# One load of r per batch, six tokens to a partition, in a linear-attention and token-mixing kernel on one Trainium2 core

## The chip, the cores and the metric

The kernel runs on one core of a Trainium2 chip. The metric is the device time in microseconds (us) of one execution; a time of a kernel is the median of its runs. Three runs of the kernel before gave 136.98, 137.22 and 137.23 us.

## The reference

A linear attention with a decaying state (4 batches, 8 heads, 768 tokens, head size 48) gives x; a block that mixes tokens and channels follows. All in float32 at the interface.

```python
# attention, per batch b and head h; state is D x D, D = 48
for t in range(S):                       # S = 768
    cur     = einsum('bhd,bhe->bhde', u * k[t], v[t])
    y[t]    = einsum('bhd,bhde->bhe', r[t], state + cur)
    state   = w * state + einsum('bhd,bhe->bhde', k[t], v[t])
x = y.transpose(0, 2, 1, 3).reshape(B, S, H * D)          # 4 x 768 x 384
# mixing
theta = x @ w_theta                                        # 384 x 384
y  = w_tok_r @ (x * cos(theta)) + w_tok_i @ (x * sin(theta))   # 768 x 768 over tokens
u  = x + y
out = u + relu(u @ w_ch)                                   # 384 x 384
```

## The kernel before

**Tiles.** A batch's 768 tokens are three *pairs*, each of two chunks of 128 tokens; there are 12 pairs in all (g = 0 to 11). For the pairs 0 to 6 (`PAIRS`) k and v lie two tokens of a head to a partition, for the later ones one token to a partition, one DMA per chunk. r lies two tokens to a partition in every pair. A load of one tensor for one pair (384 KB in all) goes into one of 16 load buffers `ld` of 128 x 768 float32.

**Attention, `front(b)`.** Per pair: r and k are multiplied by powers of w, which takes them to a common origin of the decay (`Rw`, `Kw`, L554 and L556, 128 x 768; "decay" below). The powers themselves are exponentials on ScalarE at the start (`kpow`, `rpow`, `kpow_c`, L399; one instruction for each of the two tokens of a partition). The products are turned so that the head dimension lies on partitions: `flip` (L489) is a row of 128 x 128 matmuls against an identity into one PSUM bank (L493) and one copy out of it (L503 on ScalarE, L504 on VectorE) into `RT` or `KT`. `scores` (L605) are K by R per head, masked by VectorE into `mAT` (L614). `outer` (L671) gives a chunk's contribution to the state; F, T and N (L713 to L727) carry the state on, and its 16-bit copies are `Sb` or `Sd` (L684 to L707). `vb` is the 16-bit cast of v (L581 ScalarE, L583 VectorE, L585 POOL). `PD` (L621) is R times K elementwise, `diag` (L638) sums it with u, `dg` (L643) takes it out of PSUM, and `yd` (L647) is that times v: the term of the token itself. The output of a pair is `states` (L747, L799), `outputs` (L760, L812) and `bonus` (L776) summed in PSUM and copied to x (L784, L786, L821).

**Mixing, `front` and `mixing(b)`.** x is turned (`flip TX`, or a transposing DMA, L510); `theta` (L835) and cos and sin (L842, L846) and z = x times both (L850, VectorE). `mix` (L901) multiplies the turned token weights `WrT`, `WiT` with z, 12 matmuls of 384 columns for each 128 tokens; `un` (L919) adds x; u is turned by a transposing DMA (L510), `chan` (L929) multiplies with w_ch, ScalarE takes the relu out (L956), POOL adds u (L959), and one DMA per pair writes 384 KB out (L977). Token weights come by casting DMAs that POOL issues (L462, float32 to 16 bits) and are turned by `flip W`. For the last pair alone u is made turned (L876), and sums end on VectorE (L945, L964).

**Order.** Every step is a task of a `Plan`, with the engines that could do it ("ways") and their planned nanoseconds. The program's order of tasks, the way of each, the PSUM banks and some extra waits are tables written out in the file (`ORDER`, `WAYS`, `BANKS`, `AFTER`): a pair (a, b) in `AFTER` makes task b wait for the end of task a on another engine. Each engine, and the queue of SyncE (SP) that issues nearly all loads, stores and transposing DMAs, works through its own tasks strictly in that order. A DMA's plan entry has the queue, the packets per DMA engine and nanoseconds per packet, such as `desc=(0, 64, 26)`. `IDLE` puts matmuls on zeros (L293) behind chosen tasks on TensorE, 128 x 512 ("wide") or 128 x 128 ("narrow"); `WARM` puts some at the very start. Buffers are rings, and a task that writes a buffer waits for the last readers of it:

```python
NL, NR, NK, NV, NRT, NKT, NPD, NM, NSB, ND_ = 15 if KR_BY_DMA else 16, 2, 4, 6, 4, 3, 2, 5, 6, 3
...
def load(src, b, pr, what, pairs):
    i = nload[0] % NL
    nload[0] += 1
    rows = src[b, :, 2 * pr * C:(2 * pr + 2) * C, :]
    if pairs:
        P.add(sp(lambda: nc.sync.dma_start(
            out=Ls[i].rearrange("p (h n) -> p h n", h=H),
            in_=rows.rearrange("h (p j) d -> p h (j d)", j=2))), wr=[("L", i, 0), ("L", i, 1)],
            prio=-90 + 0.001 * nload[0], desc=(0, 64, 26), name="load " + what, kind="load")
```

## Time and profile before

| | |
|---|---|
| median of 3 runs | 137.22 us (136.98 to 137.23) |
| the profiled execution | 136.61 us, of which the span from first to last instruction is 134.8 us |
| granted TensorE clock | 0.997 |
| TensorE (PE) busy | 127.9 us, 95% of the span |
| VectorE (DVE), ScalarE (ACT), GpSimd (POOL) busy | 106.1, 81.0, 68.8 us |
| DMA | 25.47 MB in 67,199 packets, 61,801 of them under 512 B |

A row of a timeline has its start and length in us, then engine, source line, operation, output<-inputs by the program's tile names, shape and count; in brackets the idle time of the engine before it and what ended it. A row of the windows view has the stretch, its length, then per engine the busy us. Matmuls are pipelined, so the length of a row of TensorE contains a drain, and the distance from start to start is what one costs in a row of them. L numbers are lines of the kernel before; the changed file is longer.

### The profile page before, as it was taken

The numbers are of one execution on the slowest core, as the hardware profiler recorded it, in microseconds if no ns is written. First come the engines' busy times: TensorE is split into PE (matmuls) and PEld (weight loads), VectorE is DVE, ScalarE is ACT, GpSimd is POOL, SyncE is SP. The second block draws the span as 40 slices with busy tenths as digits, with TensorE's granted clock in tenths as the row PEclk, the third lists the DMA queues.
The fourth block names the chain that finished last, engine by engine and source line by source line (L and its number), as shares of the span: only waits on it lengthen the run. The fifth ranks groups of instructions, "written<-read, shape, count | busy, mean of one in ns | idle before, by whom it ended". The sixth has DMA issues, their size and how long they took to land.

```text
span 134.8 us, 4625 instructions
## 1 busy us (share of the span) xinstructions
PE 127.9 (95%) x1943; PEld 85.8 (64%) x1943; DVE 106.1 (79%) x201; ACT 81.0 (60%) x157; POOL 68.8 (51%) x76
## 2 busy tenths in 40 slices
PE   6999998899999999999999999899999999999970
PEld 1346666765776775876676776566667757667840
DVE  5099988687998999889798878799899997351370
ACT  3478696598968596684965153863731758900220
POOL 6003789295160456827326989664056955370220
PEclk9999999999999999999999999999999999999998
DMA  3999999999999955797999999979899950326344
GB/s 92 265 269 261 143 204 197 255 258 234 242 277 236 261 138 74 144 209 139 281 180 234 171 189 253 163 134 309 196 302 198 103 116 8 117 79 198 78 177 173
DMA packets 67199, 25.47 MB, mean 189 GB/s; under 512 B 61801, under 2 KB 67178, under 8 KB 67178
## 3 DMA queue, kind: packets, MB, share of 16 engines
q1 hardware_dynamic: 64744, 22.23, 76.3%
q0 software_dynamic: 2432, 2.95, 13.4%
q8 instruction: 15, 0.25, 0.8%
q14 instruction: 6, 0.05, 0.1%
q10 hardware_dynamic: 2, 0.00, 0.0%
HBM read 20.06 MB, written 4.72 MB: 184 GB/s over the span
## 4 chain that ended last, share of the span: by engine, by line
PE 78%; DVE 7%; DMA 5%; ACT 2%; POOL 2%; issue 2%; DVEq 0%; POOLq 0%; ACTq 0%
PE bank L901 31%; PE bank L493 11%; PE bank L835 8%; PE bank L929 7%; DMA uu_all<-uu_all 5%; PE bank L605 4%; PE bank L876 3%; PE bank L671 3%; PE bank L760 2%; PE bank L293 2%; DVE Rw L554 2%; PE bank L747 2%; PE bank L776 1%; PE bank L812 1%; PE bank L638 1%
## 5 line engine op out<-in xcount | busy, mean ns | idle before, releaser
L901 PE MATMUL bank<-z,WrT 128*128 128x384 bf16 x132 | 43.0, 326 | 0.0
L901 PE MATMUL bank<-z,WiT 128*128 128x384 bf16 x132 | 42.9, 326 | 0.0
L959 POOL TENSOR_TENSOR fin_all<-fin_all,uu_all 128x384 f32<-128x384 f32 x20 | 19.5, 992 | 22.7 <-ACT fin_all L956 8.7
L647 POOL TENSOR_TENSOR yd<-dg,vb 128x768 bf16<-128x768 f32 x10 | 14.7, 1471 | 11.8 <-DVE PD L621 5.1
L614 DVE TENSOR_TENSOR mAT<-bank,mask 128x512 bf16<-128x512 f32 x28 | 18.4, 682 | 0.3 <-PE bank L605 0.2
L901 PEld LDWEIGHTS <-WrT 128*128 128x128 bf16 x132 | 12.9, 98 | 7.7 <-issue 0.3
L956 ACT ACTIVATE fin_all<-bank 128x384 f32<-128x384 f32 x20 | 9.7, 494 | 12.9 <-issue 8.5
L901 PEld LDWEIGHTS <-WiT 128*128 128x128 bf16 x132 | 12.9, 98 | 7.1
L919 DVE TENSOR_TENSOR uu_all<-bank,x 128x384 bf16<-128x384 f32 x22 | 11.7, 553 | 5.3 <-PE bank L901 5.1
L842 ACT ACTIVATE trig<-bank,pi 128x384 f16<-128x384 f32 x24 | 13.4, 582 | 3.2 <-PE bank L835 3.2
L835 PE MATMUL bank<-Wth,xT 128*128 128x384 bf16 x72 | 14.3, 326 | 0.0
L850 DVE TENSOR_TENSOR z<-x,trig 128x1536 bf16<-128x1536 bf16 x12 | 11.4, 952 | 3.5 <-ACT trig L842 1.8
L846 ACT ACTIVATE trig<-bank 128x384 f16<-128x384 f32 x24 | 11.3, 490 | 4.5 <-PE bank L835 4.5
L929 PE MATMUL bank<-Wch,uu_all 128*128 128x384 bf16 x69 | 13.3, 326 | 0.4 <-DMA uu_all<-uu_all 0.4
L614 DVE TENSOR_TENSOR mAT<-bank,mask_c 128x512 bf16<-128x512 f32 x20 | 13.1, 682 | 0.0
L293 PE MATMUL bank<-zero 128*128 128x512 bf16 (+1 forms) x47 | 11.8, 377 | 1.3 <-DVE zero L300 1.3
L503 ACT ACTIVATE RT<-bank 128x1024 bf16<-128x1024 bf16 x10 | 10.2, 1022 | 4.2 <-PE bank L493 4.2
L554 POOL TENSOR_TENSOR Rw<-ld,rpow 128x768 bf16<-128x768 f32 x5 | 9.0, 1810 | 5.1 <-DVE z L850 4.4
L621 POOL TENSOR_TENSOR PD<-RT,KT 128x1024 bf16<-128x1024 bf16 x4 | 8.5, 2120 | 5.9 <-DVE RT L504 4.5
L503 ACT ACTIVATE KT<-bank 128x1024 bf16<-128x1024 bf16 x9 | 9.2, 1025 | 1.9 <-PE bank L493 1.8
L554 DVE TENSOR_TENSOR Kw<-ld,kpow 128x768 bf16<-128x768 f32 x7 | 6.7, 950 | 3.6 <-ACT kpow L399 3.6
L605 PE MATMUL bank<-RT,KT 64*64 64x128 bf16 (+1 forms) x304 | 8.8, 219 | 0.0
(122 smaller groups left out, 231.2 us busy)
## 6 DMA issues: line engine op xcount, KB each, us to landing
ld<-in_r_dram SPq DMA_DIRECT2D x12, 384.0 KB, 5.7
out_dram<-fin_all SPq DMA_DIRECT2D x11, 384.0 KB, 2.5
ld<-in_k_dram SPq DMA_DIRECT2D x7, 384.0 KB, 6.0
ld<-in_v_dram SPq DMA_DIRECT2D x7, 384.0 KB, 6.1
ld<-in_k_dram SPq DMA_DIRECT2D x10, 192.0 KB, 4.6
ld<-in_v_dram SPq DMA_DIRECT2D x10, 192.0 KB, 4.7
uu_all<-in_moe_w_tok_r_dram POOLq DMA_DIRECT2D x1, 384.0 KB, 5.3
fin_all<-in_moe_w_tok_i_dram POOLq DMA_DIRECT2D x1, 384.0 KB, 6.3
```

Of the source, the lines that this page charges most:

```text
L293: ins = [nc.tensor.matmul(bank_t[k][:, :wide * C].rearrange("p (a c) -> p a c", a=wide), zero, bc(zero, 1, wide), start=True, stop=True, s ...
L493: ins = [nc.tensor.matmul(bank16(tok)[:, i * C:(i + 1) * C], s, ident, is_transpose=True, start=(i == 0), stop=(i == n - 1)) for i, s in e ...
L503: P.add([act(n * C, lambda: nc.scalar.activation(dst, src(), Act.Copy)), dve(n * C, lambda: nc.vector.tensor_copy(dst, src()), 1.0 if pair ...
L554: return eng.tensor_mul(to.rearrange("p j h d -> p h j d")[:, :, :, :D], tokens(i), pw)
L605: ins.append(nc.tensor.matmul(to[:, hp * C:(hp + 1) * C], a, m, start=(hp == 0), stop=(hp == HP - 1), skip_group_check=True))
L614: mask01[:, j] if pairs else mask_c): nc.vector.tensor_mul(
L647: return eng.tensor_mul(yd.rearrange("p a b d -> p (a b) d"), wide(dg, D), vb.rearrange("p a b d -> p (a b) d"))
L835: ins = [nc.tensor.matmul(bank(th)[:, :HD], xT[:, t, dk, :], Wth[:, dk, :], start=(dk == 0), stop=(dk == ND - 1)) for dk in range(ND)]
L842: P.add(act(HD, lambda th=th, t=t, trig=trig: nc.scalar.activation(trig[:, t, 0], bank(th)[:, :HD], Act.Sin, bias=pi2), 144), use=[th], rd ...
L901: ins.append(nc.tensor.matmul(bank(tm)[:, :HD], (WrT, WiT)[ri][:, so, to * C:(to + 1) * C], z[:, so, ri], start=(part == 0 and i == 0), st ...
L929: ins = [nc.tensor.matmul(bank(tf)[:, :HD], uT[:, t, dk, :], Wch[:, dk, :], start=(dk == 0), stop=(dk == ND - 1)) for dk in range(ND)]
L959: P.add(pool(900, lambda t=t, un=un, fin=fin: nc.gpsimd.tensor_add(fin[:, t], fin[:, t], un[:, t])), rd=[("un", j, t)], wr=[("fin", j, t)] ...
```

## The change

For the batches 1, 2 and 3 (`R6`) the whole r of a batch, 768 tokens, comes in one DMA of 1,152 KB, six tokens of a head to a partition (1,152 B in one piece instead of 384 B), into three neighbouring load buffers. There are 12 load buffers instead of 16, as one tile. Batch 0 keeps its loads. The first decay of r in such a batch waits for all of the load; the three decays of a batch write one tile `Rw6`, and four flips per batch (one for each two heads, six blocks of 128 columns) replace three (eight blocks); `RT` is per batch, [128, 4 x 768], two of them. The powers for six tokens, `rpow6`, are six more exponentials at the start on ScalarE (384 columns each) after five small VectorE operations and a POOL iota; batch 0's `rpow` lies in the second `RT` tile. PD and others read `RT` with a stride between heads. The planned packet times of DMAs are other numbers (24 for 26, 16.8 for 17.3, 76 for 87, 85 for 90, 66 for 70; the r load 53). `ORDER`, `WAYS`, `BANKS`, `AFTER` and `IDLE` are new throughout: 755 tasks instead of 747. At the start 5 matmuls on zeros in `WARM` and none in `IDLE` stand where 4 and 1 stood; behind the first flip there are 28 such matmuls instead of 36. By the new `WAYS`, VectorE has 196 tasks instead of 184 (among them 5 instead of 2 yd, 10 instead of 8 PD, 4 instead of 2 copies of r's flips, one of the last pair's two copies of u's flips), POOL 67 instead of 68, ScalarE 158 as before.

```diff
-WARM, WARM_NS = (4, 6), (855, 1280)
+WARM, WARM_NS = (5, 6), (1070, 1280)
+R6, R6_NS = (1, 2, 3), 53
...
-    NL, NR, NK, NV, NRT, NKT, NPD, NM, NSB, ND_ = 15 if KR_BY_DMA else 16, 2, 4, 6, 4, 3, 2, 5, 6, 3
+    NL, NK, NV, NKT, NPD, NM, NSB, ND_ = 12, 4, 6, 3, 2, 5, 6, 3
-    Ls = ring(NL, [C, 2 * HD], F32, "ld")
-    Rws = ring(NR, [C, 2, H, Dp], BF16, "Rw")
+    ld_all = sb.tile([C, NL * 2 * HD], F32, name="ld_all")
+    Ls = [ld_all[:, 2 * HD * i:2 * HD * (i + 1)] for i in range(NL)]
+    Rw6 = sb.tile([C, NCH, H, Dp], BF16, name="Rw6")
+    Rws = [Rw6[:, 2 * i:2 * i + 2] for i in range(NP)]
+    rpow6 = sb.tile([C, H, NCH, D], F32, name="rpow6")
...
-    RTs = ring(NRT, [C, 2 * HP * C], BF16, "RT")
+    RT6s = ring(2, [C, HP * S], BF16, "RT6")
+    rpow = RT6s[1][:, :4 * HD].bitcast(F32).rearrange("p (h j d) -> p h j d", h=H, j=2)
...
+        for j in range(NCH) if R6 else ():
+            P.add((ACT, 510, False, lambda j=j: nc.scalar.activation(
+                rpow6[:, :, j, :], lw_f, Act.Exp, scale=tok6[:, 0, j:j + 1])),
+                rd=["lw_f", "tok6"], wr=[("rpow6", j), ("exp", 10 + j)],
+                prio=-197 + 0.1 * j, name="pow6")
...
     def load(src, b, pr, what, pairs):
-        i = nload[0] % NL
         nload[0] += 1
+        if what == "r" and b in R6:
+            if pr:
+                return None
+            if slot[0] % NL + NP > NL:
+                slot[0] += NL - slot[0] % NL
+            i = slot[0] % NL
+            slot[0] += NP
+            P.add(sp(lambda: nc.sync.dma_start(
+                out=ld_all[:, 2 * HD * i:2 * HD * (i + NP)].rearrange("p (h n) -> p h n", h=H),
+                in_=src[b].rearrange("h (p j) d -> p h (j d)", j=NCH))),
+                wr=[("L", i + m, c) for m in range(NP) for c in range(2)],
+                prio=-90 + 0.001 * nload[0], desc=(0, 64, R6_NS), name="load " + what,
+                kind="load")
+            return i
+        i = slot[0] % NL
+        slot[0] += 1
...
+            if b in R6 and pr == 0:
+                t6 = ld_all[:, 2 * HD * ir:2 * HD * (ir + NP)].rearrange(
+                    "p (h j d) -> p h j d", h=H, j=NCH)
+                for m in range(NP):
+                    def decay6(eng, m=m, t6=t6):
+                        return eng.tensor_mul(
+                            Rws[m].rearrange("p j h d -> p h j d")[:, :, :, :D],
+                            t6[:, :, 2 * m:2 * m + 2, :], rpow6[:, :, 2 * m:2 * m + 2, :])
+                    P.add([dve(2 * HD, lambda f=decay6: f(nc.vector), port=True),
+                           pool(1800, lambda f=decay6: f(nc.gpsimd))],
+                          rd=[("L", ir + n, c) for n in range(NP) for c in range(2)] +
+                          [("rpow6", 2 * m + c) for c in range(2)], wr=[("Rw", m)], prio=pb,
+                          name="rw")
+                for hp in range(HP):
+                    flip(RT6[:, NCH * C * hp:NCH * C * (hp + 1)].rearrange("p (a t j) -> p a t j", a=1, j=NCH),
+                         [Rw6[:, j, 2 * hp:2 * hp + 2, :].rearrange("p h d -> p (h d)")
+                          for j in range(NCH)], ("TR", g, hp), pb,
+                         [("Rw", m) for m in range(NP)],
+                         [("RT", b % 2, m, hp) for m in range(NP)], paired=NCH)
```

In the new order batch 0's loads are issued as k, r, r, k, r, k, v, v, v; the first load of batch 1 is its r. Batch 0's first v is cast on ScalarE (POOL before), the third decay of its r is on POOL (VectorE before), and that decay is told by `AFTER` to wait for the first PD.

More of the change, by code (lines that the diff above doesn't have):

```diff
@@ L395, in setup @@
                 (rpow_c, "rpow_c", 0, 7), (rpow_c, "rpow_c", 1, 8))):
-            if dst is None:
+            if dst is None or (nm == "rpow" and 0 in R6):
                 continue
@@ L424, in setup @@
         P.add((ACT, 1290, False, lambda: nc.scalar.preload_act_table_set("trig_and_small")),
-              rd=[("exp", i) for i in range(10) if KR_BY_DMA or i not in (6, 7)], wr=["sin"], prio=-195, name="sin set")
+              rd=[("exp", i) for i in range(16 if R6 else 10)
+                  if (KR_BY_DMA or i not in (6, 7)) and
+                  (0 not in R6 or i not in (2, 3))], wr=["sin"], prio=-195, name="sin set")
         def uw_fill():
@@ L450, in load @@
                     in_=rows.rearrange("h (c p) d -> c p h d", c=2)[c])), wr=[("L", i, c)],
-                    prio=-90 + 0.001 * nload[0], desc=(0, 64, 17.3), name="load " + what,
+                    prio=-90 + 0.001 * nload[0], desc=(0, 64, 16.8), name="load " + what,
                     kind="load")
@@ L751, in states @@
                     return ins[0], ins[-1]
-                P.add(pe(340 if before else 170, states), rd=[kRT] + kS + sc, acq=ty,
+                P.add(pe(340 if before else 170, states), rd=kRT + kS + sc, acq=ty,
                       spare=1, prio=pb + 5, name="states")
@@ L803, in states @@
                     return ins[0], ins[-1]
-                P.add(pe(210 if before else 105, states), rd=[kRT] + kS + sc, acq=ty,
+                P.add(pe(210 if before else 105, states), rd=kRT + kS + sc, acq=ty,
                       spare=1, prio=pb + 5, mode=ROWS, name="states")
```

101 lines of the change are left out of this document (66 added, 35 removed), and 95 rows, old and new, of tables (AFTER, IDLE, ORDER).

## The prediction

> **What bounds the kernel now.** I read the page first, then the windows view in stretches, then TensorE's timeline up to the first mixing matmul, then the other engines' timelines over the same stretch, then the DMA part and the waits.
>
> ```profile
> span 134.8 us, 4625 instructions
> PE 127.9 (95%) x1943; PEld 85.8 (64%) x1943; DVE 106.1 (79%) x201; ACT 81.0 (60%) x157; POOL 68.8 (51%) x76
> ...
> 20.00:31.00 11.00, 10.04 (x241) 7.36 (x239) 8.81 (x18) 8.31 (x20) 7.68 (x9) 1.00 1.10 236
> 31.00:80.00 49.00, 49.00 (x856) 34.59 (x857) 44.24 (x74) 34.15 (x66) 25.58 (x24) 1.00 1.00 200
> 80.00:110.00 30.00, 29.60 (x395) 19.85 (x396) 27.43 (x47) 15.49 (x32) 18.43 (x16) 1.00 1.02 198
> 110.00:130.00 20.00, 20.00 (x209) 14.05 (x208) 9.69 (x18) 9.52 (x22) 8.56 (x9) 1.00 0.33 93
> ...
> PE bank L929 <- DMA uu_all<-uu_all: 0.4, 1, 0.4
> ```
>
> In a window row the first figure is its length, then busy us of TensorE (PE), weight loads, VectorE (DVE), ScalarE (ACT), GpSimd (POOL), then the granted clock, DMA share and GB/s. From 31 to 130 us TensorE stands still for 0.4 us, once, at a transposing DMA. VectorE is 91% busy from 31 to 110 ((44.24 + 27.43) / 79) and holds nobody up. So the last 100 us cost what TensorE's matmuls cost, and the DMA traffic that the change makes cheaper lies under them. Time can only be won before 31 us:
>
> ```profile
> 7.96 0.61 PE L493 MATMUL bank<-ident,Kw 128*128 128x128 bf16 x8
> 8.40 0.43 PE L293 MATMUL bank<-zero 128*128 128x512 bf16 x2
> ...
> 22.05 0.66 PE L747 MATMUL bank<-Sd,RT 128*128 128x96 bf16 x8
> 22.64 0.54 PE L760 MATMUL bank<-vb,mAT 64*128 64x48 bf16 x29
> 23.98 0.22 PE L760 MATMUL bank<-vb,mAT 64*128 64x48 bf16 x3 [0.80 <-issue]
> ...
> 30.95 0.32 PE L901 MATMUL bank<-z,WrT 128*128 128x384 bf16 x1
> ```
>
> The first real work starts at 7.96, the first mixing matmul at 30.95. Between them stand 36 matmuls on zeros (L293), put where the order expects a wait: 18 wide ones at 0.43 / 2 = 0.21 us and 18 narrow ones. They and the 0.80 are TensorE's reserve.
>
> **TensorE's work.** The changed order has 28 such fillers after the first flip, 16 wide and 12 narrow. The real matmuls are as many as before (r's flips are 4 x 6 blocks a batch instead of 3 x 8), but more of them come before the first mix: 1 flip of 8 blocks, 2 theta, 3 of r's 6-block flips for batch 1, 1 flip of x more and 1 of the weights fewer.
>
> ```profile
> 54.09 0.45 PE bank L493 x8
> ...
> 39.21 0.34 PE bank L493 x6
> 29.30 0.17 PE bank L293 x3
> ...
> 51.60 0.49 PE bank L835 x3
> ```
>
> That is 0.45 + 2 x 0.49 + 3 x 0.34 = 2.45 us moved ahead (a narrow filler is 0.17 / 3 = 0.06). So **the break-even is a first mix at 30.95 + 2.45 = 33.4 us**: earlier is a gain, later a loss, one to one, since all behind it is TensorE's. The fillers alone give 2 x 0.21 + 6 x 0.06 = 0.8 us, but only where the other engines are early enough to close the holes.
>
> **The start, walked.** I follow the changed order with spacings (start to start) from these rows:
>
> ```profile
> 8.60 1.02 ACT L503 ACTIVATE KT<-bank 128x1024 bf16<-128x1024 bf16 x1 [0.77 <-PE bank L493]
> 9.54 1.02 ACT L503 ACTIVATE RT<-bank 128x1024 bf16<-128x1024 bf16 x1
> 10.46 0.61 ACT L399 ACTIVATE kpow_c<-z,tok_f 128x384 f32<-128x384 f32 x1
> 10.97 0.16 ACT L419 ACTIVATE lwu<-bank 128x4 f32<-128x4 f32 x1
> 17.55 1.28 ACT L424 ACT_TABLE_LOAD   x1
> ...
> 7.87 1.83 DVE L554 TENSOR_TENSOR Rw<-ld,rpow 128x768 bf16<-128x768 f32 x2
> 14.07 0.69 DVE L621 TENSOR_TENSOR PD<-RT,KT 128x1024 bf16<-128x1024 bf16 x1
> 14.68 0.95 DVE L554 TENSOR_TENSOR Rw<-ld,rpow 128x768 bf16<-128x768 f32 x1
> 17.01 2.48 DVE L614 TENSOR_TENSOR mAT<-bank,mask 128x512 bf16<-128x512 f32 x4
> ...
> 12.19 0.82 POOL L585 CAST vb<-ld 128x768 bf16<-128x768 f32 x1 [9.54 <-DVE wup L416]
> 17.72 1.47 POOL L647 TENSOR_TENSOR yd<-dg,vb 128x768 bf16<-128x768 f32 x1
> 30.99 1.80 POOL L554 TENSOR_TENSOR Rw<-ld,rpow 128x768 bf16<-128x768 f32 x1 [0.62 <-DVE z L850]
> ...
> L581 ACT ACTIVATE vb<-ld 128x768 bf16<-128x768 f32 x6 | 5.1, 846 | 1.6 <-DMA ld<-in_v_dram 1.6
> L399 ACT ACTIVATE kpow<-z,tok_f 128x384 f32<-128x384 f32 x2 | 1.1, 608 | 0.0
> ```
>
> So an eviction of 1,024 columns takes 0.93 on ScalarE, a power 0.51, a v cast 0.8; on VectorE a decay (Rw, Kw) takes 0.9, PD 0.61, mAT 0.62. Added: six powers for six tokens (6 x 0.51 = 3.1 us of ScalarE) and five tiny VectorE operations, which with the clearing of Sd and the place matrices now stand ahead of the first decay, where VectorE waited anyway; that frees 1.2 us of its queue after it. The third r decay goes to POOL (1.8).
> ScalarE from 8.60: K0, R0, power, R1, K1, 2 powers: 13.9. R2 then waits for POOL's decay, which is told to wait for the first PD: VectorE's 2 r decays, masks, K1 decay and PD end at 11.6, POOL at 13.5, the flips at 13.95. R2, K2 (its decay stands behind PD and three mAT, 14.35; evicted 15.0 to 15.9), diagonal 16.1, power, diagonal, power, 17.4, and only then batch 0's first v cast (vb), which POOL did at 12.19 before: it ends at 18.2 by spacings, at 19.3 if all eleven steps take their mean durations. Outer products, F, Sd: first `states` at 19.35 (17.58 before), but scores and flips of all three pairs lie ahead of it, so TensorE has by then done as much as before at that time. Its second `states`, after N on VectorE, stands at 21.9, with 0.15 us less done than before at that time.
> From there the order has few holes: theta needs the table load (1.28), which stands behind the x evictions and ends at 25.3, and the copy of x's flips on VectorE, 24.6. The W casts have some 6 us each from issue to flip; they took 5.3 to 8.6 before (rows below) under heavier traffic, as the load queue stands still from 10 to 18 us in the walk. TensorE goes on to batch 1's r flips at 29 and to the first mix at 32.0; with the same small holes that the 22.05 to 30.95 stretch has besides its 0.80 (`states` takes 0.59 and not 0.35, 22.05 to 22.64), 32.8. I take the middle, 32.5: **0.9 us won**. VectorE's extra work (yd, PD, copies of r: about 6 us) is nearly all in this stretch: 7 decays 6.3, 12 mAT 7.4, 3 PD 1.8 and 14 others at the 0.6 that 44.24 / 74 gives, 8.4, make 24 us between 6.9 and 32, so about 1 us of holes is allowed. After the mix starts its load is as before.
>
> **The DMA part.**
>
> ```profile
> q1 hardware_dynamic: 64744, 22.23, 76.3%
> q0 software_dynamic: 2432, 2.95, 13.4%
> ...
> ld<-in_v_dram SPq DMA_DIRECT2D x7, 384.0 KB, 6.1
> uu_all<-in_moe_w_tok_r_dram POOLq DMA_DIRECT2D x1, 384.0 KB, 5.3
> x<-in_moe_w_tok_i_dram POOLq DMA_DIRECT2D x1, 384.0 KB, 8.6
> ...
> DMA to landing us min/median/max: 3.2/5.0/10.1
> ```
>
> A packet of q1 takes 0.763 x 16 x 134.8 / 64,744 = 25.4 ns (two tokens are 384 B); one of q0 119 ns, for 1,213 B written and twice that read as float32. A batch of r was 3,072 packets, 4.9 us of all 16 engines; it becomes 1,024 of 1,152 B, not under 25 ns and not over 119: 1.6 to 7.6 us. By bytes read on q0 (119 x 1,152 / 2,426 = 57 ns) it is 3.6, and I take that: 1.2 us saved per batch, all of it under TensorE's work, so 0 in the sum. The first such load waits for vb0 (slots 10 and 11 don't hold three, so it wraps onto the first three buffers): issued at 18.2, it lands 1.6 us of latency (3.2 less 1,024 x 25.4 / 16 = 1.6 of transfer) and 3.6 of transfer later, 23.4; VectorE wants it at 25.1.
> [...]
>
> With 12 buffers the loads have less time. Adding TensorE's rows between a load's place in the order and its first reader's: before, a full 384 KB load after the first stretch has at least 7 us against the 6.1 us row; now batch 1's second v has 4.3 and its third 3.6. The reader may wait 0 to 2.5 us each; ScalarE and VectorE then hold up what is queued behind (theta's sines, evictions), TensorE has mixing queued. With two thirds of the queue's traffic I expect landings near 4.5 us, and take **0.3 lost**.
>
> **The tail.**
>
> ```profile
> 128.29 0.17 PE bank L493 x3
> ...
> 129.38 0.50 ACT uu_all L503
> ...
> 130.37 0.55 DVE fin_all L964
> ```
>
> After the last mixing matmul (128.29) the end takes 2.63 us to 130.92, on ScalarE's copies of u and VectorE's sums. One of the two copies, 0.50 on ScalarE, goes to VectorE and stands in line with the sums there, while the waiting for ScalarE falls away: between 0 and 0.5, **0.2 lost**.
>
> Sum: -0.9 + 0.3 + 0.2 = -0.4 us. The profiled execution took 136.61 us (span 134.8, 1.8 around it), so it would be 136.2; the runs' median is 137.22, 0.6 above the profiled one, so **136.8**. About 0.2%, 0.27 us, is what a measurement can tell from no change.
>
> **Rivals.**
> *The v cast slips (slower).* ScalarE's queue is the place: with mean durations vb0 ends at 19.3, and outer products, F, Sd and the r load all hang on it. It decides from 0.7 us of slip. At 1.1 us, and 0.8 more as VectorE's 24 us of queue get holes, the mix starts at 34.4: 136.8 + 1.9 = 138.7. For it: nothing else feeds the first outer product, and the slack is nil. Against: four fillers stand in front of it. 0.17.
> *The r load is late (slower).* At 119 ns a packet it lands at 27.4 (18.2 + 1.6 + 7.6), 2.3 us after VectorE wants it, and VectorE stands in line behind it: 139.1. It decides from about 95 ns (0.7 us late). All three decays are written to wait for the whole load. Against: 57 ns by the bytes. 0.06. [...]
> *Loads late in the middle (slower).* The two v casts wait their full 1.8 and 2.5 us, half of it reaches TensorE: 136.8 - 0.3 + 2.15 = 138.65. For: rows of 6.1 us. Against: fewer packets. 0.17.
> *Fillers are only exchanged for holes (same):* the gain equals the two losses, 137.2. 0.12.
> *The forecast,* 135.4 to 136.95: 0.48. Its good end is the 32.0 mix without the two losses (-1.4) and 0.4 of those holes closed.
>
> The likeliest time is 136.8. Range: 135.4, below which I leave one in ten, to 139.1, which takes in the slower rivals at their prices. Faster 0.48, same 0.12, slower 0.40, from these cases.
>
> **What would show it.** Right: the first mix (the line of 128x384 matmuls on z) before 33.4, near 32.5; vb0 on ScalarE ended by about 18.5; r's big load landing in 5 to 6 us; TensorE 49 of 49 busy from 31 to 80. Wrong: a mix after 33.4; waits of ScalarE or VectorE on v loads over 1 us each; TensorE idle past 31 at anything but a transposing DMA; VectorE waiting on r.

## The result: 140.84 us, 2.65% slower

Four runs of the changed kernel took 139.84, 140.59, 141.09 and 141.45 us, the median is 140.84; the kernel before took 137.12 beside them (four runs, 136.98 to 137.23). The ratio is 1.0265, 95% interval 1.0201 to 1.0328. The prediction was 136.8, with a range up to 139.1: the change went the other way, and the time lies outside the range. Executions more than 1.5% above the fastest of their kernel are left out of the ratios, while the medians are of all executions.

The profiled execution is the fastest of the four. Page and windows view of the changed kernel:

```profile
span 138.1 us, 4621 instructions
PE 128.0 (93%) x1935; PEld 85.0 (62%) x1935; DVE 111.6 (81%) x217; ACT 77.7 (56%) x157; POOL 63.8 (46%) x76
...
31.00:80.00 49.00, 45.84 (x788) 31.81 (x785) 44.00 (x75) 29.37 (x58) 23.00 (x23) 1.00 1.09 219
40.00:45.00 5.00, 3.51 (x80) 2.00 (x78) 4.23 (x8) 0.54 (x2) 4.86 (x5) 1.00 1.18 139
45.00:50.00 5.00, 3.89 (x98) 3.10 (x102) 2.58 (x6) 2.69 (x4) 1.20 (x2) 1.00 1.15 322
```

From 31 to 80 us TensorE was busy 49.00 of 49 us before and is busy 45.84 now: 3.16 us idle, where the forecast had none. The span grew by 3.3. The start, which was to bring the gain, came as walked (timeline):

```profile
17.64 0.86 ACT L659 ACTIVATE vb<-ld_all 128x768 bf16<-128x768 f32 x1
...
32.79 0.33 PE L979 MATMUL bank<-z,WrT 128*128 128x384 bf16 x1
```

The first mix is at 32.79, 0.6 us ahead of the break-even of 33.4. The loss stands near 45 us, in two places of TensorE's timeline, with the VectorE row on which the second one hangs:

```profile
45.06 0.51 PE L538 MATMUL bank<-ident,x 128*128 128x128 bf16 x6 [1.55 <-DMA x<-in_moe_w_tok_i_dram]
48.72 0.33 PE L825 MATMUL bank<-Sd,RT 128*128 128x96 bf16 x4 [1.05 <-DVE Sd L773]
...
47.39 0.56 DVE L661 CAST vb<-ld_all 128x768 bf16<-128x768 f32 x1 [2.59 <-DMA ld_all<-in_v_dram]
```

TensorE waits 1.55 us for a casting load of weights and 1.05 us for `Sd`, the 16-bit state. `Sd` takes 0.24 us on VectorE, but is queued there behind the cast `vb` of batch 1's second v, and that cast waits 2.59 us for its load. Both late loads hang on SyncE's queue (timeline, then waits of SyncE's queue and of GpSimd):

```profile
18.93 0.68 SPq L487 DMA_DIRECT2D ld_all<-in_k_dram  x1
...
29.81 0.37 SPq L493 DMA_DIRECT2D ld_all<-in_v_dram  x1
...
38.83 1.32 SPq L555 DMA_TRANSPOSE uu_all<-uu_all  x1
40.21 0.60 SPq L487 DMA_DIRECT2D ld_all<-in_v_dram  x1
40.85 0.96 SPq L476 DMA_DIRECT2D ld_all<-in_r_dram  x1
...
SPq L493 <- DMA ld_all<-in_r_dram: 6.3, 1, 6.3
SPq L493 <- POOL Rw L616: 3.8, 1, 3.8
...
POOL z L507 <- DMA ld_all<-in_k_dram: 6.8, 1, 6.8
```

From 19.6 to 29.8 us SyncE issues nothing. At the head of its queue stands half a v load of batch 2 (L493, 192 KB), first read at 74.4 us. It goes into one of the three buffers of batch 1's r, and as six tokens of a head lie in one piece, such a buffer comes free only when all three decays have read. Three loads of batch 1 stand behind it. The second k lands near 36.6; GpSimd is told by `AFTER` to wait for it (the 6.8 us) before it issues the last two of the six casting loads of token weights. The second v stands further behind, after a transposing DMA, is issued at 40.21 and lands 7.2 us later.

The new order also moved these casting loads. The one that TensorE waits for here is the third of Wi that goes into `x`; GpSimd issued it at 15.31 before and issues it at 37.33 now (GpSimd's timeline, before, then changed):

```profile
15.31 0.74 POOL L462 DMA_DIRECT2D x<-in_moe_w_tok_i_dram  x1
```

```profile
37.33 0.72 POOL L507 DMA_DIRECT2D x<-in_moe_w_tok_i_dram  x1
```

The prediction has no term for that, and no run puts this load back to its early place.

The DMA part of the page:

```profile
q1 hardware_dynamic: 58504, 22.23, 77.2%
...
ld_all<-in_r_dram SPq DMA_DIRECT2D x3, 1152.0 KB, 8.0
ld_all<-in_v_dram SPq DMA_DIRECT2D x7, 384.0 KB, 6.2
```

The packets are 6,240 fewer, the bytes and the queue's share (76.3% before) are not less. A v load lands in 6.2 us, as late as before (6.1).

### The profile page after: what moved, and what is told of

It reads as the page before. It is cut to its first block, busy times and chain, and to the rows that moved or that the text cites. A ratio compares the mean times of both kernels' runs of the same rounds, so it can differ in the third digit from the quotient of the medians.

```text
span 138.1 us, 4621 instructions
## 1 busy us (share of the span) xinstructions
PE 128.0 (93%) x1935; PEld 85.0 (62%) x1935; DVE 111.6 (81%) x217; ACT 77.7 (56%) x157; POOL 63.8 (46%) x76
## 3 DMA queue, kind: packets, MB, share of 16 engines
q1 hardware_dynamic: 58504, 22.23, 77.2%
## 4 chain that ended last, share of the span: by engine, by line
PE 56%; DVE 18%; DMA 13%; POOL 4%; ACT 3%; issue 3%; DVEq 0%; SPq 0%; POOLq 0%
PE bank L979 20%; DMA ld_all<-in_v_dram 9%; PE bank L913 7%; PE bank L538 6%; PE bank L299 4%; PE bank L1007 3%; PE bank L954 3%; PE bank L683 3%; DVE z L928 3%; DVE mAT L692 3%; POOL fin_all L1037 3%; DMA ld_all<-in_k_dram 3%; PE bank L838 2%; PE bank L854 2%; DVE Kw L608 2%
## 5 line engine op out<-in xcount | busy, mean ns | idle before, releaser
L1037 POOL TENSOR_TENSOR fin_all<-fin_all,uu_all 128x384 f32<-128x384 f32 x20 | 17.8, 913 | 21.2 <-ACT fin_all L1034 12.6
L692 DVE TENSOR_TENSOR mAT<-bank,mask 128x512 bf16<-128x512 f32 x28 | 18.2, 681 | 0.6 <-PE bank L683 0.5
L920 ACT ACTIVATE trig<-bank,pi 128x384 f16<-128x384 f32 x24 | 14.2, 595 | 3.2 <-PE bank L913 2.9
L725 POOL TENSOR_TENSOR yd<-dg,vb 128x768 bf16<-128x768 f32 x7 | 10.3, 1470 | 4.2 <-ACT dg L721 2.0
L616 POOL TENSOR_TENSOR Rw<-ld_all,rpow 128x768 bf16<-128x768 f32 x5 | 9.0, 1806 | 7.0 <-PE bank L683 4.6
L299 PE MATMUL bank<-zero 128*128 128x512 bf16 (+1 forms) x39 | 11.0, 402 | 1.1 <-DVE zero L306 1.1
L548 ACT ACTIVATE KT<-bank 128x1024 bf16<-128x1024 bf16 x8 | 8.2, 1028 | 6.5 <-PE bank L538 6.5
L548 ACT ACTIVATE RT<-bank 128x768 bf16<-128x768 bf16 (+1 forms) x11 | 9.7, 878 | 0.3 <-PE bank L538 0.3
L1007 PEld LDWEIGHTS <-uu_all 128*128 128x128 bf16 x69 | 6.2, 97 | 3.9 <-DMA uu_all<-uu_all 0.4
L913 PEld LDWEIGHTS <-xT 128*128 128x128 bf16 x72 | 6.0, 97 | 3.8 <-DMA xT<-x 0.4
```

The source lines that it names most:

```text
L299: ins = [nc.tensor.matmul(bank_t[k][:, :wide * C].rearrange("p (a c) -> p a c", a=wide), zero, bc(zero, 1, wide), start=True, stop=True, s ...
L548: P.add([act(n * C, lambda: nc.scalar.activation(dst, src(), Act.Copy)), dve(n * C, lambda: nc.vector.tensor_copy(dst, src()), 1.0 if pair ...
L692: mask01[:, j] if pairs else mask_c): nc.vector.tensor_mul(
L913: ins = [nc.tensor.matmul(bank(th)[:, :HD], xT[:, t, dk, :], Wth[:, dk, :], start=(dk == 0), stop=(dk == ND - 1)) for dk in range(ND)]
L920: P.add(act(HD, lambda th=th, t=t, trig=trig: nc.scalar.activation(trig[:, t, 0], bank(th)[:, :HD], Act.Sin, bias=pi2), 144), use=[th], rd ...
L1007: ins = [nc.tensor.matmul(bank(tf)[:, :HD], uT[:, t, dk, :], Wch[:, dk, :], start=(dk == 0), stop=(dk == ND - 1)) for dk in range(ND)]
```

## The experiments

Task names in the edits: k11 is the k load of batch 1's pair 1 (counted from 0), and so on. An edit of `ORDER` moves the named tasks, all else stays. Each run had 6 executions or more beside the kernel before, whose medians were 136.8 to 137.1.

### Places in the queue, a cast's wait, packet size

**ahead_two**

```diff
 ORDER: ... k12,
+  v11, r2,
   ... turn TU ...,
-  v11, ... r2,
```

> The changed kernel with two loads moved ahead in the written order and nothing else: the second v load of batch 1 and the r load of batch 2 stand directly behind the third k load of batch 1, ahead of the transposing DMA that stood before them. Theory 1 (the loss is the place of the loads in SyncE's in-order queue): that v load is issued near 35 us instead of 40.2, lands before 43 instead of at 47.39, the wait of 2.59 us of its cast goes, TensorE's stretch 45 to 50 us fills up from 3.89 to about 4.8 us, and the time falls by 0.8 to 1.5 us, to about 139.5. Theory 2 (the r load of 1,152 KB itself clogs the queue, wherever it stands): it now stands in front of as much as before, and the time stays within 0.4 us of 140.8. Theory 3 (VectorE's extra work is the bound): no change either, within 0.3 us.

Measured: 142.93 us (142.51 to 145.29), ratio 1.0474 (1.0402 to 1.0546). Slower than the changed kernel, against all theories. Timeline and windows:

```profile
47.33 0.60 PE L538 MATMUL bank<-ident,x 128*128 128x128 bf16 x6 [2.88 <-DMA x<-in_moe_w_tok_i_dram]
...
45.00:50.00 5.00, 2.67 (x20) 2.00 (x21) 2.80 (x6) 1.17 (x2) 3.06 (x4) 0.76 1.22 240
```

The v load is early now and TensorE waits 1.3 us longer than before this edit for GpSimd's casting load (2.88 against 1.55). From 45 to 50 us, the stretch with most of that wait, TensorE's granted clock is 0.76.

**ahead_all**

```diff
 ORDER: every load behind the first mix
+  9.5 us of TensorE's work ahead of its first reader (r: 12), as far as its buffers allow
-  with 3.6 us and more
```

> The changed kernel with every load behind the first mix moved ahead in the written order, to where TensorE has about 9.5 us of work (12 us for an r load) between the load's place and its first reader, as far as the 12 buffers allow; transposing DMAs, outputs and all other steps stand as they were. Theory 1 (place in SyncE's queue): most of the idle time of TensorE between 40 and 80 us goes and the time falls by 2 to 3.5 us, to 137.3 to 138.8. Theory 2 (the r loads' transfers): less than 0.6 us is won. Theory 4 (the 12 buffers bind): less than 1 us is won, since loads that wait for a buffer can't move.

Measured: 139.06 us (138.61 to 142.91), ratio 1.0160 (1.0099 to 1.0221). 1.8 us won, a little less than theory 1 expected: the best of all changed versions, and still slower than before. DMAs on the load buffers from 18 to 48 us, first of the changed kernel, then of this one:

```profile
DMA to landing us min/median/max: 5.0/7.3/10.1
```

```profile
DMA to landing us min/median/max: 5.8/9.7/14.5
```

Issued earlier, the loads take longer to land (median 9.7 us against 7.3), so a part of the lead is lost again. And the loads that come sooner hold up the start (TensorE's timeline of this kernel):

```profile
30.65 0.84 PE L538 MATMUL bank<-ident,fin_all 128*128 128x128 bf16 x12 [0.72 <-DMA fin_all<-in_moe_w_tok_i_dram]
```

TensorE waits for an earlier casting load of weights, and the first mix stands at 34.21; in the trace of the changed kernel whose first flip is as slow (after_again, below) there is no such wait, and it stands at 33.56. The same shows in far_back_v_ahead below: a wait of 0.80 us there, and the first mix at 33.53 instead of 32.79 with equally fast first flips.

**cast_free**

```diff
 AFTER:
-  (k11, cast of Wr on GpSimd),
+  (k10, cast of Wr on GpSimd),
```

> The changed kernel with one ordering wait exchanged: the first cast load of Wr on GpSimd waits for the first k load of batch 1, landed near 25 us, instead of for the second, landed near 36.6. Theory 1b (these casts, held to a late load, cost the 1.6 us that TensorE idles at 43.2 us): the time falls by 0.7 to 1.6 us. Rival (the next late load, the second v of batch 1 at 47.39 us, is issued by SyncE whatever TensorE does, so that the idle time only moves there): within 0.4 us of 140.8, and the flips' gap of 1.6 us is gone while the one at 47.4 us grows by about as much.

Measured: 144.11 us (142.46 to 145.27), ratio 1.0508 (1.0438 to 1.0577), the slowest. Timeline and windows:

```profile
42.36 1.04 PE L538 MATMUL bank<-ident,Kw 128*128 128x128 bf16 x8 [3.06 <-DVE Kw L608]
...
40.00:45.00 5.00, 2.64 (x28) 1.68 (x28) 3.63 (x5) 0.84 (x1) 0.80 (x1) 0.63 0.62 146
```

The trace is of the slowest execution, 145.27 us. Now the casts are early and the k load behind them late: TensorE waits 3.06 us for the decay of k, and the clock falls to 0.63 (40 to 45 us). The mirror image of ahead_two.

**r_in_384B**

```diff
-  one DMA of r, [p, h, 6 x 48]
+  three DMAs of r, [p, h, 2 x 48] each, same buffers and layout
```

> The changed kernel with each r load of batches 2 to 4 written as three DMAs of 384 bytes to a packet, for the same layout and buffers: 3,072 packets a load instead of 1,024. By the prediction's estimate (57 ns for a packet of 1,152 bytes, 24 to 29 ns for one of 384) each r load takes 1.0 to 2.0 us longer and the time rises by 0.3 to 1.5 us. If a large packet costs in proportion to its bytes (about 75 to 85 ns), the load's landing stays near 8.0 us and the time within 0.4 us of 140.8: then the larger packets buy nothing, and theory 2 in the form 'packets of 1,152 bytes clog the queue' falls too unless the time comes out lower.

Measured: 142.48 us (140.50 to 145.34), ratio 1.0338 (1.0259 to 1.0418). That is 1.6 us more than the changed kernel by the medians, but against its second set of executions (ratio 1.0334, after_again) no difference can be told: the large packets do no harm that this run could show, and what they win is not measured. The packet records of the two traces give 58.2 ns for the mean packet of 1,152 B and 27 ns for one of 384 B: 3.7 against 5.2 us of all DMA engines for a batch of r.

### Is it one load, one transfer, or the DMA engines?

**far_load_back**

```diff
 ORDER: ...
-  v21 (half),
   k11, v10, k12, ... v20,
+  v21 (half),
```

> The changed kernel with one half load moved back in the written order and nothing else: a v load of batch 2's second pair (192 KB, first read 41 us of TensorE's work later), which stood on SyncE's queue ahead of three loads of batch 1 and there waited for all decays of batch 1's r, so that SyncE issued nothing from 19.6 to 29.8 us, goes behind the loads of batch 2's first pair. Theory 5 (this wait at the head of the queue is the loss: a far load in one of r's three buffers, which come free only when all three decays have read them): the three k and v loads of batch 1 are issued from about 20 us, GpSimd's casts no longer wait 6.8 us for one of them, the gap of 1.7 us at 43.2 us goes, and 1.5 to 3 us are won: 137.8 to 139.3. Theory 6 (the DMA engines are full from 20 to 50 us anyway, so that a load issued earlier only queues elsewhere): less than 0.6 us is won.

Measured: 140.86 us (139.51 to 142.09), ratio 1.0290 (1.0225 to 1.0355): nothing won. Theory 5 falls as a price, though its mechanism went as said: the loads are issued from 20.6 us. Rows of GpSimd, ScalarE and TensorE:

```profile
41.93 1.80 POOL L608 TENSOR_TENSOR Kw<-ld_all,kpow 128x768 bf16<-128x768 f32 x1 [8.85 <-DMA ld_all<-in_k_dram]
...
46.84 0.36 ACT L770 ACTIVATE Sd<-N 64x192 bf16<-64x192 f32 x1 [5.21 <-POOL N L804]
...
48.84 0.33 PE L825 MATMUL bank<-Sd,RT 128*128 128x96 bf16 x4 [1.46 <-ACT WrT L548]
71.07 0.66 PE L913 MATMUL bank<-Wth,xT 128*128 128x384 bf16 x3 [1.55 <-DMA xT<-x]
```

The third k load is issued at 26.7 and GpSimd's decay waits for it until 41.9; the state step N stands behind that decay, ScalarE waits 5.21 us for N, and the copies of WrT that release `states` stand behind ScalarE's `Sd`: TensorE waits 1.46 us at the same place as before. Its wait for the casting load near 45 us is gone, but one of 1.55 us for a transposing DMA at 71.07 is new.

**far_back_v_ahead** and **far_back_four_ahead** (added to the last edit)

```diff
+  v11 directly behind k12                       (both)
+  r2 behind v11; v12, k20 ahead of a turn TU    (four)
```

> As the run with the far half load moved back, and the second v load of batch 1 also ahead of the transposing DMA that it stood behind, directly behind batch 1's third k load. Theory 5 with the order behind transposing DMAs as its second half: the gap of 1.2 us at 47.5 us goes too, 0.5 to 1.5 us less than with the far load alone, 136.8 to 138.5. Theory 6: no less than with the far load alone, or more, since this load then competes with GpSimd's casting loads.

> As the run before it, and the r load of batch 2, the third v load of batch 1 and the first k load of batch 2 ahead of transposing DMAs too. Theory 5: another 0 to 1 us less, since the waits on these loads were 0.7 to 3 us on ScalarE and VectorE and mostly hidden; about 136.5 to 138. Theory 6 (full DMA engines): the loads needed first land later behind the ones needed later, and the time is 0.3 us or more over that with one load moved ahead.

Measured: 140.78 us (138.87 to 142.00), ratio 1.0270 (1.0199 to 1.0341), and 139.84 (139.04 to 140.99), ratio 1.0240 (1.0185 to 1.0295). At best 1 us is won, where theory 5 gave 2.8 to 4.3.

**r2_a_third** (two thirds of batch 2's r are left out)

```diff
-  in_=r[2] [p, h, 6 x 48]
+  in_=r[2] [p, h, 2 x 48]; the three decays read these
```

> The changed kernel in which the r load of batch 2 brings only the first two of the six tokens of each partition, 384 KB instead of 1,152 (the three decays all read these; so batch 2's output leaves out two thirds of r); the order is untouched. Theory 2 (the large load clogs the queue at 40 to 49 us): the v load of batch 1 issued just ahead of it lands in about 5 instead of 7.2 us, and 0.8 to 1.6 us are won. Theories 1 and 5 (the place in the queue): that v load is still issued at 40.2 us, and within 0.4 us of 140.8.

Measured: 141.39 us (140.90 to 143.83), ratio 1.0349 (1.0300 to 1.0398): nothing won. SyncE's and VectorE's rows:

```profile
40.89 0.57 SPq L489 DMA_DIRECT2D ld_all<-in_v_dram  x1
...
48.48 0.56 DVE L663 CAST vb<-ld_all 128x768 bf16<-128x768 f32 x1 [3.15 <-DMA ld_all<-in_v_dram]
```

The v load still takes 7.6 us from issue to landing with a third of r behind it. Batch 2's large load is not what delays it: theory 2 falls for this place. (Batch 1's large load, the first one, was not varied.)

### Controls in the kernel before

**before_r_together**

```diff
 ORDER of the kernel before: v10, r10,
+  r11, r12,
   k10,
-  r11,
   v..., k11,
-  r12,
```

> The kernel before, with one thing of the change imitated in its order: the second and third r load of batch 1 (384 KB each) are issued directly behind the first, ahead of two k loads and a v load of that batch, instead of between and behind them; 16 buffers, packets of 384 bytes and all else as they were. Theory 6 (the DMA engines are full up to about 47 us, so bytes that come sooner than needed delay others that are needed): k and v of batch 1 land up to 3 us later, TensorE gets idle time between 25 and 50 us, and the time rises by 0.5 to 2.5 us. Rival (transfers lie under TensorE's work, as the prediction had it): within 0.3 us of the kernel before.

Measured: 141.56 us median; five of six executions 140.99 to 142.04, one 137.16. As the other five lie far above it, there is no ratio; the profile is of 141.92. Timeline and windows:

```profile
37.19 0.96 DVE L554 TENSOR_TENSOR Kw<-ld,kpow 128x768 bf16<-128x768 f32 x1 [3.76 <-DMA ld<-in_k_dram]
38.21 1.03 PE L493 MATMUL bank<-ident,Kw 128*128 128x128 bf16 x8 [3.12 <-DVE Kw L554]
...
35.00:40.00 5.00, 1.88 (x14) 1.29 (x13) 2.81 (x3) 1.83 (x4) 0.00 (x0) 0.82 1.03 238
40.00:45.00 5.00, 5.00 (x70) 3.68 (x68) 3.75 (x7) 2.65 (x4) 2.52 (x2) 0.84 0.86 213
```

With 16 buffers, small packets and the old engines' work, 768 KB of r brought forward past two k and one v cost 4.4 us at the median, though not in every execution: the sixth paid nothing. In the profiled one the k decay waits 3.76 us, TensorE 3.12, and its clock is 0.82 to 0.84 in the stretches from 35 to 45 us. Its first flip was slow, too (1.01 us), and its first mix is at 31.70 instead of 30.95, so about 0.75 us of this execution's loss lie ahead of the moved loads. The rival, the prediction's own "under TensorE's work", falls for this trace and, by their times, for four more executions; it held in the sixth, of which there is no trace. How much the DMA engines had to do is in the windows of the kernel before, in shorter stretches than the prediction looked at:

```profile
35.00:40.00 5.00, 5.00 (x106) 3.47 (x105) 4.79 (x8) 3.95 (x6) 2.52 (x2) 1.00 1.17 260
40.00:45.00 5.00, 5.00 (x63) 3.70 (x62) 4.53 (x10) 3.35 (x7) 0.78 (x1) 1.00 1.14 256
...
50.00:55.00 5.00, 5.00 (x77) 3.16 (x67) 4.85 (x10) 3.25 (x7) 3.79 (x6) 1.00 0.53 75
```

From 30 to 45 us the DMA share is 1.14 to 1.17 (over 1 means that records of packets on one engine overlap), from 50 to 55 it is 0.53, and from 60 to 80 again 1.07 to 1.12. The 1.00 of the long row from 31 to 80 is a mean over all of these. The share alone does not say that there is no room: from 60 to 80 us TensorE stands still nowhere, and in the changed kernel a share of 1.18 goes with 139 GB/s (40 to 45 us) and one of 1.15 with 322 GB/s (45 to 50). That the DMA engines had no room for r rests on the k load that came late in this run, not on the share.

**wi_an_eighth** and **before_wi_a_sixth** (Wi is left out of the result)

```diff
-  casting loads of Wi: 768 columns
+  96 columns, flips read Wr's (changed kernel); 128 columns, flips read these (kernel before)
```

> The changed kernel in which GpSimd's three casting loads of the weights Wi bring 96 of 768 columns, and Wi's flips read what Wr's loads brought (so Wi is left out of the result); orders, buffers and all r, k, v loads are untouched. This takes about 2 us of all DMA engines per load away, 6 us before 45 us. Theory 6 (full DMA engines up to 47 us): k and v loads land 1 to 3 us sooner, the gaps at 43 and 47 us shrink from 2.9 us to under 1, and the time falls by 1.5 to 3 us. Theory 1 (SyncE's places alone: the waits of its queue on r's decays and on VectorE stay): the gap at 43 us goes with the load it waited for, the one at 47 stays, and 0.5 to 1.2 us are won.

> Control: the kernel before with Wi's three casting loads cut to 128 of 768 columns (Wi is left out of the result). If full DMA engines cost only the changed kernel, which has waits on loads, this leaves the time within 0.4 us of the kernel before (137.1); if all kernels of this kind gain from less traffic at the start, it gains 1 us or more as the changed kernel did (1.4 us), and that gain is then no part of the change's loss.

Measured: 139.39 us (138.17 to 140.67), ratio 1.0167 (1.0101 to 1.0233), and 135.62 (135.03 to 136.47), ratio 0.9919 (0.9879 to 0.9958). The changed kernel gains 1.5 us, but so does the kernel before, where the first mix comes 0.8 us sooner (30.16). In the changed kernel's trace the wait for Wi's casting load is gone and 0.70 us of the wait for `Sd` is left. Less traffic at the start is worth some 1.5 us to either; this is no measure of the change's own loss.

### What stands behind the late load

**all_ahead_far_back** and **state_chain_first**

```diff
 ORDER of ahead_all:
+  v21 (half) behind v20; v11 behind k12                       (both)
+  GpSimd: Sd, N ahead of decay k12, PD; VectorE: Sd ahead of vb    (second)
```

> As the run with all loads moved ahead, with the far half load moved back behind batch 2's first loads, and the second v load of batch 1 directly behind the third k load. Theory 6: about the same as with all loads ahead, 139.1 within 0.6 us, as the DMA engines are full either way. Theory 5 (the far load at the head of the queue): 1 us or more below that.

> As the run just named, and on GpSimd the two small steps that carry the state on (a copy Sd and N) stand ahead of the decay of batch 1's third k and of a PD, and on VectorE another copy Sd ahead of the cast of v. In the runs with loads ahead TensorE waited 1.2 to 1.6 us near 46 to 47 us for those steps, which stood behind a decay that waited 9 us for its k load. Theory 7 (what is left of the loss at 47 us is this chain behind a late load): 0.8 to 1.5 us less than without this move, to about 138. Rival (the flip of that k waits next, as its load lands no sooner): within 0.4 us of it.

Measured: 140.20 us (138.41 to 142.76), ratio 1.0179 (1.0102 to 1.0255), and 141.95 (139.03 to 142.40; no ratio, again for one execution far below the others). By the ratio the first equals ahead_all (1.0160), as theory 6 expected, though its median lies 0.5 us above the bound given; theory 5's gain did not come. The second is worse: with N moved up, TensorE no longer waits for the state, but 2.27 us for `yd`, which then stood last on GpSimd (trace of an execution of 141.97 us).

**after_again**

> The changed kernel once more, unaltered, for a second trace of it. Open is whether the profiled execution, the fastest of its runs (139.84; the others 140.6 to 141.5), shows the whole loss. If TensorE's first flips run slow in some executions (eight matmuls of a flip in 1.01 us instead of 0.61, as in most traces of the altered kernels), the first mix comes 0.5 to 1.2 us later than 32.8 and an execution takes 140.6 to 141.5. If all executions start alike, the first mix stands within 0.2 us of 32.8.

Measured: 141.40 us (140.71 to 142.93), ratio 1.0334 (1.0271 to 1.0397). Its trace is of the slowest of the six executions, 142.93 us. Timelines and windows:

```profile
7.82 1.01 PE L538 MATMUL bank<-ident,Kw 128*128 128x128 bf16 x8
...
33.56 0.33 PE L979 MATMUL bank<-z,WrT 128*128 128x384 bf16 x1
...
48.97 0.56 DVE L661 CAST vb<-ld_all 128x768 bf16<-128x768 f32 x1 [3.40 <-DMA ld_all<-in_v_dram]
50.30 0.33 PE L825 MATMUL bank<-Sd,RT 128*128 128x96 bf16 x4 [2.61 <-DVE Sd L773]
...
31.00:80.00 49.00, 44.43 (x720) 30.80 (x718) 41.31 (x69) 29.15 (x57) 19.99 (x21) 0.97 1.05 213
45.00:50.00 5.00, 2.61 (x36) 2.18 (x36) 1.60 (x4) 2.81 (x4) 1.98 (x2) 1.00 1.21 212
50.00:55.00 5.00, 4.70 (x112) 3.13 (x113) 3.74 (x9) 1.23 (x3) 1.80 (x1) 0.66 1.23 208
```

It shows two things more than the first trace. The first flip ran slow (1.01 us for eight matmuls instead of 0.61), so the first mix is at 33.56, past the break-even: the gain of the start is gone. And the wait at 50 us is 2.61 us, after which the clock is 0.66 for 5 us: by an estimate another 0.34 x 5 = 1.7 us. The wait for `Sd` and the fall of the clock are not peculiar to this execution: the trace of warm_up_seven, below, taken at 141.19 us, has 2.32 us and 0.66.

**wi_an_eighth_all_ahead** (Wi is left out)

```diff
+  the order of ahead_all and the casting loads of wi_an_eighth
```

> The changed kernel with both reliefs at once: the order with every load ahead, and Wi's three casting loads cut to an eighth (Wi is left out of the result). If the DMA engines' debt up to 47 us and the places of the loads make up the whole loss, the time comes to 136 to 137.6, that of the kernel before. If VectorE's extra work and the chain through GpSimd carry a part of their own, it stays at 138.2 or more.

Measured: 141.04 us (139.67 to 141.94), ratio 1.0279 (1.0203 to 1.0356): worse than either relief alone, 1.6 to 2 us. Timelines of VectorE, GpSimd and TensorE:

```profile
45.64 2.92 DVE L665 CAST vb<-ld_all 128x768 bf16<-128x768 f32 x1
...
46.31 1.82 POOL L620 TENSOR_TENSOR Rw<-ld_all,rpow 128x768 bf16<-128x768 f32 x1
...
49.33 0.40 PE L829 MATMUL bank<-Sd,RT 128*128 128x96 bf16 x4 [2.46 <-DVE Sd L777]
```

Here v is in time. But r is early too, so GpSimd's decay of it falls on the cast of v, which takes 2.92 us instead of 0.56, and `Sd` behind it is late again, by 2.46 us. The time stays above the 138.2 of the second forecast, but through this new wait, so it does not say what VectorE's extra work costs by itself.

**warm_up_seven**

```diff
-WARM = (5, 6)
+WARM = (5, 7)
```

> The changed kernel with seven instead of six matmuls on zeros in the last group ahead of TensorE's first flip, so that its idle time there is 0.3 instead of 0.7 us. If that idle time lets the first flips run slow in some executions, all start alike now and the median falls by 0.3 to 0.8 us. If the slow first flips come from when the clock rises within a run of matmuls, whatever their number, nothing changes (within 0.3 us).

Measured: 141.32 us (140.81 to 143.36), ratio 1.0309 (1.0248 to 1.0369): no change, and its first flip took 1.06 us in the one trace. The idle time ahead of the first flip was not what made it slow there.

**sd_ahead_of_v** and **sd_ahead_v_early**

```diff
 ORDER on VectorE: ... mAT,
+  Sd,
   vb of v11, out W,
-  Sd,
(second: also v21 (half) behind v20, v11 behind k12)
```

> The changed kernel with one small step of VectorE moved and nothing else: the 16-bit copy Sd (0.24 us) for batch 1's second pair stands ahead of the cast of that pair's v instead of behind it. In the second trace of the changed kernel that cast waited 3.4 us for its load, TensorE's first product with Sd waited 2.6 us behind it, and then the clock fell to 0.66 for 5 us. Theory 8 (the late v load costs so much because VectorE works in order and Sd is queued behind the waiting cast): TensorE's wait at 47 us falls under 1.5 us, as the state products now run and only the outer products wait for v; the clock stays at 1.0 there and 1 to 2.5 us are won, to 138.5 to 140.3. Rival (the outer products, 1.1 us later in the order, need the same v and wait as long): within 0.5 us of the changed kernel run beside it before (141.4).

> The same move of Sd, with the far half load moved back and batch 1's second v load directly behind its third k load, so that the cast finds its data landed. Theory 8: what is left at 47 us is the chain over GpSimd (1.2 to 1.6 us in the runs with loads ahead), and 0 to 1 us more is won: 138 to 139.8. Theory 6 (full DMA engines): the v load that comes sooner delays GpSimd's casting loads by as much, and the time is that of the other run within 0.5 us.

Measured: 141.81 us (139.71 to 144.33), ratio 1.0270 (1.0209 to 1.0330), and 141.02 (138.43 to 142.56; no ratio). Timelines of VectorE and TensorE and a window of the first:

```profile
45.62 0.69 DVE L773 CAST Sd<-F 64x192 bf16<-64x192 f32 x1
48.50 0.33 PE L825 MATMUL bank<-Sd,RT 128*128 128x96 bf16 x4
...
50.00:55.00 5.00, 4.70 (x73) 3.02 (x66) 4.87 (x9) 1.75 (x4) 1.80 (x1) 1.00 1.16 188
```

In the trace theory 8 holds: `Sd` runs at 45.62, TensorE's wait for it is gone and the clock stays at 1.00. In the time it does not: the first is within 0.5 us of the changed kernel's second set (141.40). Its TensorE has its idle time elsewhere (1.64 us at the casting load, 1.15 us between 80 and 110 us). The second meets neither forecast: not 138 to 139.8, and not within 0.5 us of the first.

## Why the prediction was wrong, step by step

**Right: the start.** vb on ScalarE was expected to end at 18.2 and ends at 18.5; the first mix was expected at 32.5 and is at 32.79 in the first trace. By the break-even of 33.4 that is 0.6 us won. What the walk did not know is that the first flip's speed differs from execution to execution (0.61 us in the first trace, 1.01 in the second); in the second trace nothing is left of the gain. In the first trace the sum of what is seen is -0.6 at the start, 3.0 more idle time of TensorE from 31 to 130 us (3.40 against 0.40) and 0.3 at the end (below); of the 3.3 us that the span grew, about 0.6 show in no wait.

**Right: the packet.** 57 ns by the bytes; 58.2 measured.

**Near its price: the tail.** The last mixing matmuls and the last output of the changed kernel, then the last output of the kernel before:

```profile
130.92 0.33 PE L954 MATMUL bank<-WiT,z 128*128 128x128 bf16 x3
...
134.22 0.38 SPq L1055 DMA_DIRECT2D out_dram<-fin_all  x1
```

```profile
131.41 0.38 SPq L977 DMA_DIRECT2D out_dram<-fin_all  x1
```

From the end of the last mixing matmul to the last output it is 2.97 us (131.25 to 134.22) and was 3.12 (128.29 to 131.41; the prediction's 2.63 stopped one sum short of the end). So 0.15 us are won up to there. But from that issue to the end of the span it is 3.9 us now and was 3.4, so the end as a whole costs 0.3 where 0.2 was taken; it changes nothing.

**Wrong: "all of it under TensorE's work, so 0 in the sum".** This step failed. It priced a transfer by whether TensorE was busy above it, not by what the transfer puts off. In before_r_together, without any other part of the change, 768 KB of r brought forward made a k load late, TensorE waited 3.12 us for it in the traced execution, and five of six executions were 3.9 to 4.9 us slower. In the changed kernel itself no run isolates the price of batch 1's r load; there, each edit that made one load earlier made another one late (ahead_two, cast_free, ahead_all).

**Wrong in size: "with two thirds of the queue's traffic I expect landings near 4.5 us", 0.3 lost.** Packets fell, bytes did not: 22.23 MB on q1 either way, 77.2% of a longer span. v loads land in 6.2 us, r in 8.0 where 5 to 6 were expected; batch 1's second v takes 7.2 us (8.0 in the second trace, from the issue at 41.0). Its lead was 4.3 us of work. Where 0.3 us was taken, TensorE's wait behind that v is 1.05 us in the first trace and 2.61 in the second, before any fall of the clock. The other large wait, 1.55 and 0.80 us for the casting load of Wi, had no term at all. Together with smaller waits TensorE is idle for 3.16 us from 31 to 80 us in the first trace, and in the second one for 4.57, plus an estimated 1.5 for the clock (0.03 x 49).

**The rival "loads late in the middle"** (138.65, 0.17) named the mechanism and the load. It was under-priced: half of the wait was to reach TensorE, with mixing queued as cover. But VectorE takes its tasks in the written order: `Sd`, a step of 0.24 us that TensorE needs at once, stood behind the waiting cast (47.39) and ran at 48.33, and in the second trace the fall of the clock (0.66 from 50 to 55 us) comes on top. The rivals "the v cast slips" and "the r load late" did not happen in the first trace: the cast ended at 18.5, and VectorE came to batch 1's r only at 26.0.

**Missed: the half load at the head of SyncE's queue.** The prediction counted lead from a load's place in the order to its reader; a load that waits for buffers makes every load behind it late, whatever their places (SyncE issued nothing from 19.6 to 29.8 us). But it did not decide: with it moved, the loads were issued 7 to 10 us sooner, batch 1's third k took some 15 us to land (26.7 to 41.9), and TensorE waited elsewhere.

**What stays open.** Changed orders won at most 1.8 us of the 3.7. From 60 to 70 us VectorE is busy for all of 10 us now and for 9.24 before:

```profile
60.00:70.00 10.00, 9.88 (x214) 7.18 (x213) 10.00 (x16) 8.85 (x18) 4.99 (x6) 1.00 1.06 205
```

Whether its 5.5 us of extra work hold part of the rest was not tried, nor were more than 12 buffers in the changed kernel, nor the early place of Wi's casting load. That displaced loads can cost this much was seen in the kernel before, in five executions of six; why the sixth paid nothing, and how much of the loss in the changed kernel comes from this, stays open.

## What to carry to other kernels

Look at the DMA share and at the landing times in stretches as short as the waits that matter; a mean over 49 us hid both 1.17 and 0.53 here. A transfer under a busy engine can still have a price, that of the loads it puts off (4.4 us at the median in before_r_together), and merging loads brings bytes forward that nobody needs yet. And price a late load by the step queued behind its reader, not by the reader (here `Sd`, 0.24 us, behind a cast that waited 2.59 us).

## What the runs showed of the hardware

- **TensorE's clock after a wait.** With waits of 2.3 to 3.1 us the granted clock fell to between 0.63 and 0.82 in one of the stretches of 5 us that hold the wait or follow it (state_chain_first, warm_up_seven, wi_an_eighth_all_ahead, r2_a_third, after_again, ahead_two, cast_free, all_ahead_far_back, before_r_together); after the waits of 1.55 and 1.05 us in the first trace and of 1.64 us in sd_ahead_of_v it stayed at 1.00. The shortest wait with a fall was 2.27 us (state_chain_first, 0.66); no run varies the length of the wait alone.
- **The first flips differ by execution.** The same eight matmuls took 0.61 or 1.01 us in traces of the same kernel, and with 1.01 us the first mix came 0.8 us later (33.56 against 32.79); with one more matmul on zeros in front it was 1.06 us (warm_up_seven). No run shows what sets this.
- **A VectorE cast under GpSimd's work.** 2.92 us instead of 0.56 (wi_an_eighth_all_ahead) while GpSimd issued a casting load (45.48 to 46.29) and ran a decay (46.31 to 48.13); the cast ended at 48.56, 0.43 us after the decay. No run isolates the cause.
